# Polysketch attention and a gated FFN on one core: w_out's sums laid over 128 partitions, copies moved behind the sigmoids, and kv joined with neighbouring projections

## The chip, the cores and the metric

The kernel runs on one core of one Trainium2 chip. The metric is the device time of one execution in microseconds (us), as the median of the runs. Engines are named as in the profile: PE is TensorE (PEld its weight loads), ACT is ScalarE, DVE is VectorE, POOL is GpSimd, and SP is the engine that only issues DMAs. A queue letter behind an engine (SPq, ACTq) means its instruction queue. "Lnnn" is a line of the kernel file.

## What is computed

A kernelized attention over 4 batches, 4 heads, 1088 positions and 32 dimensions per head is followed by a feed-forward block with a sigmoid gate. In float32:

```python
def phi(x):                      # 64 features from 32 dimensions, r = 8
    a = np.einsum('rd,bhsd->bhsr', S1, x)
    b = np.einsum('rd,bhsd->bhsr', S2, x)
    return np.einsum('bhsi,bhsj->bhsij', a, b).reshape(*x.shape[:-1], r * r)
q_p, k_p = phi(q), phi(k)
kv = np.einsum('bhsf,bhsd->bhfd', k_p, v)
z = np.sum(k_p, axis=2)
num = np.einsum('bhsf,bhfd->bhsd', q_p, kv)
den = np.einsum('bhsf,bhf->bhs', q_p, z)[..., None] + 1e-06
x = (num / den)                  # reordered to 4352 tokens x 128
gate = 1.0 / (1.0 + np.exp(-(x @ w_gate)))   # 128 x 1536
out = gate * (x @ w_val) @ w_out             # 1536 x 128
```

## The kernel before

**The feed-forward part is the long one.** The 4352 tokens are cut into nine chunks: eight of 512 and a last one of 256. Within a chunk the 1536 hidden columns are cut into twelve blocks of 128. One block of one chunk is a "wave" (`w1`, matmul at L540): the gate and the value projection into one PSUM tile of two banks (pool `psm`, two buffers, tag "wave"), then a sigmoid of the gate half on ACT (L548, into `sg`), then the product of value half and sigmoid on DVE (`glu`, L583; L576 in the last chunk, where one wave holds two blocks). Waves are counted through: chunk 0 has waves 0 to 11, chunk 1 has 12 to 23, and so on; the last chunk has six, from wave 96.

**The second projection.** Chunk 0 multiplies by w_out in the plain way (`w2`, L421), and the last chunk too, with tokens as rows of the result (`w2_end`, L447, `store_end`, L403 and L405). Chunks 1 to 7 are `fast`: a pair of waves and the matching pair of w_out's blocks form a 2 by 2 block product, done with seven half-size products in place of eight (Strassen's scheme in Winograd's form). POOL forms the sums of the activations (`token_sums`, L367, tile `tsum`) and of the weights (`weight_sums`, tile `ws`). `w2_a` issues four products into PSUM bank acc0, `w2_b` three into bank acc1 (L377, both in pool `pso`, one buffer for each bank). They accumulate over the chunk's six pairs. Behind the last pair the banks are summed: ACT copies the upper 64 partitions of a bank to the lower ones (`other`, L473 and L502), DVE adds on 64 partitions (`add`, L479), two transposes (L514) make rows of tokens, and four DMAs (eight where a chunk reaches into the next batch) store them from `o_sb` (L389, on SP). The sum steps are put into the list `moe["late"]`, from which each slot takes one (two in the last chunk).

**The order is written out by hand** for PE, DVE, ACT and POOL (`manual_schedule`, L65): each engine runs what the Python code issues to it, in that order. Only the order of SP's DMAs is chosen by the scheduler. The unit of order is `slot(group, waves)`: it issues an attention step (`group`), then `glu` of the wave before, one entry of `late`, the products that are due (`todo`: `w2_a` three and `w2_b` four waves behind the pair's second wave, each one earlier for the last pair of chunk 7, the flag `early`), and last a new wave with its sigmoid.

**The attention part** of batch 0 runs ahead of the waves. That of batches 1 to 3 is spread over the slots; `plan` gives, for batches 2 and 3, the wave number of each step. `turn_k` and `turn_q` transpose the inputs. `begin` projects keys (`kps`, L673) into the PSUM tile "two" (pool `ps2`, one buffer) and queries (`qcomp`, L819), whose result goes by a DMA on ACT's queue (L837) into a DRAM tile `dq` of one buffer; from there `spread` reads it back with repetition on SP's queue (L844 for the tiles qp and bq, further rows for the tiles a8 and b8). `outer` (L752) makes key features, `sum_z` their sums. `kv_all` is `kv` (L892 and L901, into a PSUM tile "two") and `kvd`, a copy on ACT (L914). `ndt` transposes it on PE (L948, copied at L965), `weights_z` makes the weights of the denominator on DVE (L1001, L1007, L1008), `qmult` (L872) makes query features, and `parts` computes the denominators (`den_j`, L1021) and numerators (L1258), divides, and writes the token columns `xT` that the waves read. `load_kq` and `load_v` fetch the next batch's inputs on SP's queue into the pool `ld`, where one buffer serves kq and bq in turn.

The heart of a slot, as it stands before the change:

```python
            glu()
            for _ in range(2 if moe["ci"] >= len(tok_chk) - 1 else 1):
                if moe["late"]:
                    moe["late"].pop(0)()
            while todo and todo[0][0] <= moe["n"]:
                todo.pop(0)[1]()
            if behind is not None:
                behind()
                behind = None
            if more:
                w1()
```

The end of the program stores the last 256 tokens from two tiles of the ring that `o_sb` uses (pool `sbA`, two buffers):

```python
        o_sb = [sbA.tile([P, P], F32, tag="o_sb", name="o_end") for _ in range(2)]
        for u, copy in enumerate((nc.scalar.copy, nc.vector.tensor_copy)):
            copy(out=o_sb[u], in_=acc[u])
```

Of the kernel before, what the change touches and what calls it, by code (L numbers as in the profile page):

```python
# [16 lines left out]
P = 128  # L17
# [3 lines left out]
def kernel(  # L21
# [24 lines left out]
    NJK = 9  # L46
# [9 lines left out]
    sbN = ctx.enter_context(tc.tile_pool(name="sbN", bufs=1))  # L56
    sbG = ctx.enter_context(tc.tile_pool(name="sbG", bufs=3))

# [288 lines left out]
    moe = {"sum": -1, "ci": 0, "w": 0, "n": 0, "ready": 0, "acc": None, "gate": None, "todo": [], "late": []}  # L347
# [17 lines left out]
    def token_sums(g, t, odd):  # L365
# [48 lines left out]
    def w2(ci, j0, jn, g):  # L414
# [13 lines left out]
        if j0 + jn == NJ:  # L428
            o_sb = sbA.tile([P, 2, TCH // 32, 32], F32, tag="o_sb", name="o_sb")[:, 0]
# [29 lines left out]

    def w2_a(ci, i, g, t):  # L460
# [3 lines left out]
        lo, hi = fst["a"][:64], fst["a"][64:]  # L464
        w, first, last = w_sb[:, 2], i == 0, i == NJ // 2 - 1
        product(lo[:, :HALF], w[:, 2 * i, :64], g[:, 0, :HALF], first, last)
        product(hi[:, :HALF], w[:, 2 * i + 1, :64], g[:, 1, :HALF], first, last)
        product(lo[:, HALF:], ws[:, 3, i], g[:, 1, HALF:], False, last)
        product(hi[:, HALF:], ws[:, 1, i], t[:, 2], False, last)
        if last:  # L470
            e = fst["e"] = raw.tile([P, 2, 2, HALF], F32, tag="w_in", name="other")[:64]
            r = fst["r"] = raw.tile([P, 6, HALF], F32, tag="w_in", name="res")[:64]
            nc.scalar.copy(out=e[:, 0], in_=hi.rearrange("p (u x) -> p u x", u=2))  # L473

            add(ends(r, 1, 3), twice(lo[:, :HALF]), e[:, 0])
            moe["late"] += [lambda: add(r[:, 2], lo[:, HALF:], r[:, 4])]

    def add(out, in0, in1, op=ALU.add):
        nc.vector.tensor_tensor(out=out, in0=in0, in1=in1, op=op)  # L479

    def twice(x):
        return bass.AP(tensor=x.tensor, offset=x.offset, ap=[list(x.ap[0]), [0, 2], [1, HALF]])

    def ends(r, u, step):
        x = r[:, u]
        return bass.AP(
            tensor=x.tensor, offset=x.offset, ap=[list(x.ap[0]), [step * HALF, 2], [1, HALF]]
        )

    def w2_b(ci, i, g, t):  # L490
        if i == 0:
            fst["b"] = pso.tile([P, TCH], F32, tag="acc1", name="prod")
        lo, hi = fst["b"][:64], fst["b"][64:]
        w, first, last = w_sb[:, 2], i == 0, i == NJ // 2 - 1
        p5 = (lo[:, :HALF], ws[:, 0, i], t[:, 0], first, last)
        p4 = (hi[:, :HALF], w[:, 2 * i + 1, 64:], t[:, 3], first, last)
        p7 = ((hi if i % 2 else lo)[:, HALF:], ws[:, 2, i], t[:, 1], False, i >= NJ // 2 - 2)
        for p in (p4, p5, p7) if i % 2 else (p5, p4, p7):
            product(*p)
        if last:  # L500
            e, r = fst["e"], fst["r"]
            nc.scalar.copy(out=e[:, 1], in_=hi.rearrange("p (u x) -> p u x", u=2))  # L502
# [900 lines left out]
```

## Time and profile before

| what | value |
|---|---|
| median of 3 runs | 292.83 us (292.31 to 293.69) |
| the profiled execution's own time | 296.02 us |
| its span in the trace | 294.1 us |
| PE busy | 288.8 us |
| DVE busy | 186.5 us |
| POOL busy | 160.6 us |
| ACT busy | 93.7 us |
| HBM read and written | 20.60 MB and 3.26 MB |
| granted TensorE clock | 0.999 of full |

How to read it: a group line gives the line, engine, operation and tiles, then "busy us, mean ns of one | idle time of that engine just before, and what ended most of it". A timeline line gives start and duration in us, with the engine, the line, the tiles, and in brackets how long the engine had been idle and who released it. Spans of matmuls overlap a little because weight loads and column halves run beside each other. The profiled execution is 1.1% longer than the median; times of single instructions are from it.

### The profile page before, as it was taken

Reading aid. Unit: us, or ns where it says so; the run is one execution under the profiler, and the core shown is the slowest. Engines: PE = TensorE matmul, PEld = TensorE weight load, DVE = VectorE, ACT = ScalarE, POOL = GpSimd, SP = SyncE. Lnnn points to the kernel's source line nnn. Section 1 sums busy time; section 2 is a strip of 40 time slices with the busy share of each in tenths; the row PEclk is TensorE's granted clock in tenths of the full one; section 3 lists DMA queues with packets and bytes.
Section 4 is the critical chain, followed back from the end, with each engine's and each line's share of the span. In section 5 each row is a group of like instructions: output and inputs, shape, how many; then the busy total and the mean of one; then the engine's idle time right before and its main releaser. Section 6 shows DMA issues by size and latency. Waiting matters only on the chain.

```text
span 294.1 us, 5762 instructions
## 1 busy us (share of the span) xinstructions
PE 288.8 (98%) x2264; PEld 156.6 (53%) x2264; DVE 186.5 (63%) x316; ACT 93.7 (32%) x172; POOL 160.6 (55%) x222
## 2 busy tenths in 40 slices
PE   8989999999999999999999999999999999999995
PEld 3543433355455455545555555554555555555895
DVE  5778789885656766677556696667436423552482
ACT  3386542321324222323224222323223223322321
POOL 2266544796535657655456498555456565646300
PEclk9999999999999999999999999999999999999999
DMA  7993613295640168416000474202000200020003
GB/s 219 347 336 68 150 39 125 74 180 137 186 97 0 19 163 159 133 50 177 12 0 2 129 174 106 37 0 38 1 0 2 36 2 0 0 31 7 0 4 54
DMA packets 28890, 24.23 MB, mean 82 GB/s; under 512 B 18560, under 2 KB 24064, under 8 KB 28864
## 3 DMA queue, kind: packets, MB, share of 16 engines
q1 hardware_dynamic: 25808, 21.95, 30.1%
q10 hardware_dynamic: 3056, 1.92, 2.3%
q8 instruction: 18, 0.29, 0.4%
q14 instruction: 8, 0.07, 0.1%
HBM read 20.60 MB, written 3.26 MB: 81 GB/s over the span
## 4 chain that ended last, share of the span: by engine, by line
PE 89%; DMA 7%; SPq 1%; DVE 0%; issue 0%; ACT 0%; DVEq 0%
PE wave L540 55%; PE prod L377 20%; DMA bq<-dq 5%; PE moeout L421 4%; PE moeout L447 2%; PE warm L297 1%; PE kps L673 1%; SPq L844 1%; PE nps L1258 1%; DMA s_in<-in_S_dram 1%; PE kvz L892 1%; PE cqps L819 1%; DMA dq<-cq 1%; DMA b<-dq 1%; PE denj L1021 0%; PE dps L1063 0%
## 5 line engine op out<-in xcount | busy, mean ns | idle before, releaser
L540 PE MATMUL wave<-xT,w_sb 128*64 128x512 f32 (+3 forms) x820 | 210.6, 566 | 0.0
L540 PEld LDWEIGHTS wave<-xT,w_sb 128*64 128x64 f32 (+1 forms) x820 | 85.4, 140 | 63.2 <-issue 51.0
L548 ACT ACTIVATE sg<-wave 128x512 f32<-128x512 f32 x102 | 60.9, 597 | 171.1 <-PE wave L540 163.2
L583 DVE TENSOR_TENSOR g<-wave,sg 128x512 f32<-128x512 f32 x96 | 65.9, 686 | 76.3 <-ACT sg L548 75.0
L367 POOL TENSOR_TENSOR tsum<-g 128x256 f32<-128x256 f32 x84 | 67.9, 810 | 29.7 <-DVE g L583 29.6
L367 POOL TENSOR_TENSOR tsum<-g,tsum 128x256 f32<-128x256 f32 x42 | 34.2, 814 | 57.8 <-DVE g L583 57.6
L377 PE MATMUL prod<-tsum,ws 128*64 128x256 f32 x252 | 62.8, 381 | 0.0
L377 PEld LDWEIGHTS prod<-tsum,ws 128*64 128x64 f32 x252 | 31.2, 137 | 16.0 <-issue 11.8
L377 PE MATMUL prod<-g,w_sb 128*64 128x256 f32 x168 | 34.7, 381 | 0.0
L367 POOL TENSOR_TENSOR tsum<-tsum,g 128x256 f32<-128x256 f32 x42 | 32.7, 779 | 3.3
L377 PE MATMUL prod<-tsum,w_sb 128*64 128x256 f32 x84 | 25.3, 383 | 0.0
L377 PEld LDWEIGHTS prod<-g,w_sb 128*64 128x64 f32 x168 | 16.0, 136 | 17.5 <-issue 14.7
L377 PE MATMUL prod<-g,ws 128*64 128x256 f32 x84 | 25.0, 379 | 0.0
L117 POOL TENSOR_TENSOR head<-head,tail 128x384 int32<-128x384 int32 (+1 forms) x10 | 9.9, 987 | 13.9 <-DVE head L111 12.6
L377 PEld LDWEIGHTS prod<-g,ws 128*64 128x64 f32 x84 | 11.5, 137 | 3.7
L421 PE MATMUL moeout<-g,w_sb 128*128 128x512 f32 (+1 forms) x28 | 12.5, 603 | 0.0
L377 PEld LDWEIGHTS prod<-tsum,w_sb 128*64 128x64 f32 x84 | 10.8, 137 | 3.0 <-issue 2.2
L872 DVE TENSOR_TENSOR qp<-qp,bq 128x1152 f32<-128x1152 f32 (+1 forms) x7 | 9.4, 1344 | 4.6 <-DMA a<-dq 4.6
L752 DVE TENSOR_TENSOR kp<-kab 128x1152 f32<-128x1152 f32 (+2 forms) x10 | 10.9, 1101 | 0.0
L576 DVE TENSOR_TENSOR g<-wave,sg 128x512 f32<-128x512 f32 x6 | 6.7, 1121 | 4.6 <-ACT sg L548 4.6
L479 DVE TENSOR_TENSOR res<-prod,other 64x512 f32<-64x512 f32 (+1 forms) x14 | 7.6, 544 | 3.1 <-DMA a<-dq 1.6
L514 DVE STREAM_TRANSPOSE o_sb<-res 64x512 f32<-64x512 f32 x14 | 9.6, 688 | 0.0
(129 smaller groups left out, 209.6 us busy)
## 6 DMA issues: line engine op xcount, KB each, us to landing
qp<-dq SPq DMA_DIRECT2D x7, 576.0 KB
bq<-dq SPq DMA_DIRECT2D x14, 288.0 KB
kq<-in_k_dram SPq DMA_DIRECT2D x3, 544.0 KB
kq<-in_q_dram SPq DMA_DIRECT2D x3, 544.0 KB
w_in<-in_moe_w_out_dram SPq DMA_DIRECT2D x6, 256.0 KB
w_in<-in_moe_w_gate_dram SPq DMA_DIRECT2D x5, 256.0 KB
w_in<-in_moe_w_val_dram SPq DMA_DIRECT2D x5, 256.0 KB
v<-in_v_dram SPq DMA_DIRECT2D x8, 144.0 KB
```

The source lines that it names most:

```text
L117: nc.gpsimd.tensor_tensor(out=head, in0=head, in1=tail, op=ALU.add)
L367: nc.gpsimd.tensor_tensor(out=t[:, u], in0=in0, in1=in1, op=ALU.subtract)
L377: nc.tensor.matmul(out=out, lhsT=lhsT, rhs=rhs, start=start, stop=stop, skip_group_check=True)
L421: nc.tensor.matmul(out=moe["acc"][d], lhsT=w_sb[:, 2, j, d], rhs=g[:, jj], start=(j == 0), stop=(j == NJ - 1),)
L479: nc.vector.tensor_tensor(out=out, in0=in0, in1=in1, op=op)
L514: nc.vector.transpose(out=o_sb[:64, d].rearrange("p t x -> p (t x)"), in_=r[:, 1 + 2 * d : 3 + 2 * d].rearrange("p u x -> p (u x)"),)
L540: nc.tensor.matmul(out=wv[d, which, jj * tw + o : jj * tw + o + tp], lhsT=w_sb[:, which, j0 + jj, d], rhs=xT[:, t0 + o : t0 + o + tp], sta ...
L548: nc.scalar.activation(out=sg, in_=wv[:, 0], func=ACTF.Sigmoid)
L576: nc.vector.tensor_tensor(out=g.rearrange("p (j u s y) -> p j y u s", j=2, u=2, y=4), in0=wv[:, 1].rearrange("p (j y u s) -> p j y u s", j ...
L583: nc.vector.tensor_tensor(out=g, in0=wv[:, 1], in1=sg, op=MUL)
L752: eng.tensor_tensor(out=KP[b][:, pi, j0:j1].rearrange("p j m (i l) -> p (j m) i l", i=R), in0=bass.AP(tensor=a0.tensor, offset=a0.offset, ...
L872: nc.vector.tensor_tensor(out=q0, in0=q0, in1=half(BQ[b], n), op=MUL)
```

## The change

It has five parts.

1. The seven products go to other halves of the two banks: the sums behind the last pair run on 128 partitions, with the first half of the output columns on the lower 64 and the other half on the upper 64. The copies between partition halves are 64x256 each, made by `cross` on ACT; there are three behind `w2_a`'s last pair, three behind `w2_b`'s, and one of a sum. DVE makes two dependent adds from acc0 (`shared`), two more from acc1 (`first_half`), one for the second half, and one 128x512 transpose. `o_sb` has half its former size. `token_sums` forms t[1] ahead of t[3].
2. The copies are collected in `moe["copies"]` and issued behind the new wave's sigmoid of the slot, in place of ahead of it.
3. The flag `early` goes; a flag `behind` makes the first pair of chunk 1 one wave later.
4. kv of batch 2 is issued into the same PSUM tile as the key projections of batch 3 (`begin(3, 2)`), and kv of batch 3 into the tile of batch 2's last numerators (`parts(2, 3)`). `plan` is replaced by a written-out order, in which batch 3 begins at wave 36 in place of 53 and its parts stand at wave 56 in place of 68; batch 2's begin stands at wave 27 in place of 31.
5. `load_kq(2)` and `load_kq(3)` are issued earlier, into a tile of a new pool that takes the place of `sbN` once that is closed. A warming matmul of 64 columns has 128.

The diff, without blank lines:

```diff
@@
     ld = ctx.enter_context(tc.tile_pool(name="ld", bufs=1))
     sbA = ctx.enter_context(tc.tile_pool(name="sbA", bufs=2))
     raw = ctx.enter_context(tc.tile_pool(name="raw", bufs=NJ // 2))
-    sbN = ctx.enter_context(tc.tile_pool(name="sbN", bufs=1))
     sbG = ctx.enter_context(tc.tile_pool(name="sbG", bufs=3))
+    top = ExitStack()
+    sbN = top.enter_context(tc.tile_pool(name="sbN", bufs=1))
     dram = ctx.enter_context(tc.tile_pool(name="dram", bufs=1, space=bass.MemoryType.DRAM))
@@
     k_t, q_t = {}, {}
+    late_pool = []
     def new_kq(b):
-        t = ld.tile([P, 2 * H * W1], F32, tag="kq", name="kq")
+        pool, tag, w = (ld, "kq", 2 * H * W1) if b < 2 else (late_pool[0], "kq2", 2 * T * D)
+        t = pool.tile([P, w], F32, tag=tag, name="kq")
         kq = t[:, : 2 * T * D].rearrange("p (a t d) -> p a t d", a=2, t=T)
         k_t[b], q_t[b] = kq[:, 0], kq[:, 1]
@@
     xT = const.tile([P, NTOK], F32, tag="xT")
-    moe = {"sum": -1, "ci": 0, "w": 0, "n": 0, "ready": 0, "acc": None, "gate": None, "todo": [], "late": []}
+    moe = {"sum": -1, "ci": 0, "w": 0, "n": 0, "ready": 0, "acc": None, "gate": None, "todo": [], "late": [], "copies": []}
     def fast(ci):
         return 0 < ci < len(tok_chk) - 1 and tok_chk[ci][1] == TCH
@@
             sub(0, g[:, 0, HALF:], g[:, 0, :HALF])
             return
         sub(2, g[:, 1, HALF:], t[:, 0])
-        sub(3, t[:, 2], g[:, 1, :HALF])
         sub(1, g[:, 1, HALF:], g[:, 0, HALF:])
+        sub(3, g[:, 1, :HALF], t[:, 2])
     def product(out, lhsT, rhs, start, stop):
         nc.tensor.matmul(
...
@@
     fst = {}
     def w2_a(ci, i, g, t):
         if i == 0:
             moe["sum"] = ci
             fst["a"] = pso.tile([P, TCH], F32, tag="acc0", name="prod")
-        lo, hi = fst["a"][:64], fst["a"][64:]
+        ps = fst["a"]
+        lo, hi = ps[:64], ps[64:]
         w, first, last = w_sb[:, 2], i == 0, i == NJ // 2 - 1
         product(lo[:, :HALF], w[:, 2 * i, :64], g[:, 0, :HALF], first, last)
-        product(hi[:, :HALF], w[:, 2 * i + 1, :64], g[:, 1, :HALF], first, last)
+        product(hi[:, :HALF], ws[:, 1, i], t[:, 2], first, last)
         product(lo[:, HALF:], ws[:, 3, i], g[:, 1, HALF:], False, last)
-        product(hi[:, HALF:], ws[:, 1, i], t[:, 2], False, last)
+        product(hi[:, HALF:], ws[:, 2, i], t[:, 1], False, last)
         if last:
-            e = fst["e"] = raw.tile([P, 2, 2, HALF], F32, tag="w_in", name="other")[:64]
-            r = fst["r"] = raw.tile([P, 6, HALF], F32, tag="w_in", name="res")[:64]
-            nc.scalar.copy(out=e[:, 0], in_=hi.rearrange("p (u x) -> p u x", u=2))
-            add(ends(r, 1, 3), twice(lo[:, :HALF]), e[:, 0])
-            moe["late"] += [lambda: add(r[:, 2], lo[:, HALF:], r[:, 4])]
-    def add(out, in0, in1, op=ALU.add):
-        nc.vector.tensor_tensor(out=out, in0=in0, in1=in1, op=op)
-    def twice(x):
-        return bass.AP(tensor=x.tensor, offset=x.offset, ap=[list(x.ap[0]), [0, 2], [1, HALF]])
-    def ends(r, u, step):
-        x = r[:, u]
-        return bass.AP(
-            tensor=x.tensor, offset=x.offset, ap=[list(x.ap[0]), [step * HALF, 2], [1, HALF]]
-        )
+            e = fst["e"] = raw.tile([P, 4, HALF], F32, tag="w_in", name="other")
+            r = fst["r"] = raw.tile([P, 3, HALF], F32, tag="w_in", name="res")
+            cross(e[:64, 0], hi[:, :HALF])
+            cross(e[64:, 0], lo[:, :HALF])
+            cross(e[:64, 1], lo[:, :HALF])
+            def shared():
+                add(r[:, 0], ps[:, :HALF], e[:, 0])
+                add(r[:, 0], ps[:, HALF:], r[:, 0])
+                cross(e[64:, 1], r[64:, 0])
+            moe["late"] += [shared]
+    def cross(out, in_):
+        moe["copies"].append(lambda: nc.scalar.copy(out=out, in_=in_))
+    def add(out, in0, in1):
+        nc.vector.tensor_tensor(out=out, in0=in0, in1=in1, op=ALU.add)
     def w2_b(ci, i, g, t):
         if i == 0:
             fst["b"] = pso.tile([P, TCH], F32, tag="acc1", name="prod")
-        lo, hi = fst["b"][:64], fst["b"][64:]
+        ps = fst["b"]
+        lo, hi = ps[:64], ps[64:]
         w, first, last = w_sb[:, 2], i == 0, i == NJ // 2 - 1
-        p5 = (lo[:, :HALF], ws[:, 0, i], t[:, 0], first, last)
+        p5 = (lo[:, HALF:], ws[:, 0, i], t[:, 0], False, last)
         p4 = (hi[:, :HALF], w[:, 2 * i + 1, 64:], t[:, 3], first, last)
-        p7 = ((hi if i % 2 else lo)[:, HALF:], ws[:, 2, i], t[:, 1], False, i >= NJ // 2 - 2)
-        for p in (p4, p5, p7) if i % 2 else (p5, p4, p7):
+        out2 = hi[:, HALF:] if i % 2 else lo[:, :HALF]
+        p2 = (out2, w[:, 2 * i + 1, :64], g[:, 1, :HALF], first, i >= NJ // 2 - 2)
+        for p in (p4, p5, p2) if i % 2 else (p2, p4, p5):
             product(*p)
         if last:
             e, r = fst["e"], fst["r"]
-            nc.scalar.copy(out=e[:, 1], in_=hi.rearrange("p (u x) -> p u x", u=2))
-            o_sb = sbA.tile([P, 2, TCH // 32, 32], F32, tag="o_sb", name="o_sb")
-            def fifth_seventh():
-                add(ends(r, 2, 3), twice(lo[:, :HALF]), ends(r, 2, 2))
-                add(r[:, 0], lo[:, HALF:], e[:, 1, 1])
-            def last_sums():
-                add(r[:, 3], r[:, 4], e[:, 1, 0], op=ALU.subtract)
-                add(r[:, 3:5], ends(r, 3, 2), twice(r[:, 0]))
-            def turned(d):
+            cross(e[:64, 2], lo[:, HALF:])
+            cross(e[64:, 2], lo[:, HALF:])
+            cross(e[:64, 3], hi[:, HALF:])
+            o_sb = sbA.tile([P, TCH // 32, 32], F32, tag="o_sb", name="o_sb")
+            def first_half():
+                add(r[:, 1], ps[:, :HALF], e[:, 1])
+                add(r[:64, 1], r[:64, 1], e[:64, 3])
+            def turn_store():
                 nc.vector.transpose(
-                    out=o_sb[:64, d].rearrange("p t x -> p (t x)"),
-                    in_=r[:, 1 + 2 * d : 3 + 2 * d].rearrange("p u x -> p (u x)"),
-                )
-            def turn_store():
-                turned(1)
-                store(ci, lambda g4: o_sb[32 * (g4 % 2) : 32 * (g4 % 2) + 32, g4 // 2])
-            moe["late"] += [fifth_seventh, last_sums, lambda: turned(0), turn_store]
+                    out=o_sb.rearrange("p t x -> p (t x)"),
+                    in_=r[:, 1:3].rearrange("p u x -> p (u x)"),
+                )
+                store(ci, lambda g4: o_sb[32 * g4 : 32 * g4 + 32])
+            moe["late"] += [first_half, lambda: add(r[:, 2], r[:, 0], e[:, 2]), turn_store]
     def w1():
@@
             token_sums(pair, moe["t"], odd)
             if odd:
                 part = (ci, j0 // 2, pair, moe["t"])
-                early = ci == len(tok_chk) - 2 and j0 == NJ - 1
-                todo.append((n + 3 - early, lambda: w2_a(*part)))
-                todo.append((n + 4 - early, lambda: w2_b(*part)))
+                behind = ci == 1 and j0 == 1
+                todo.append((n + 3 + behind, lambda: w2_a(*part)))
+                todo.append((n + 4 + behind, lambda: w2_b(*part)))
         moe["gate"] = glu
         moe["w"] += 1
@@
                 behind = None
             if more:
                 w1()
-            elif not todo:
+            for copy in moe["copies"]:
+                copy()
+            moe["copies"] = []
+            if more:
+                continue
+            if not todo:
                 break
             else:
                 todo.pop(0)[1]()
@@
     WD = 160
     mask = {}
-    def kps(b):
+    def kps(b, also=None):
         t = ps2.tile([P, 2, 512], F32, tag="two", name="kps")
+        if also is not None:
+            kv(also, ZS[also], t[:, 0, NJK * 32 : NJK * 32 + 2 * F])
         ts = [t[:, 0], t[:, 1]]
         turns = [(g, pi) for g in range(4) for pi in range(2)]
...
@@
                     skip_group_check=True,
                 )
-    def kv(b, zsum):
-        kvz = KVZ[b] = ps2.tile([P, 2, 512], F32, tag="two", name="kvz")[:, 0]
+    def kv(b, zsum, kvz=None):
+        if kvz is None:
+            kvz = ps2.tile([P, 2, 512], F32, tag="two", name="kvz")[:, 0]
+        KVZ[b] = kvz
         for j in [1, 2, 3, 4, 5, 6, 7, 8, 0]:
             for h in range(H):
                 nc.tensor.matmul(
@@
         start=True,
         stop=True,
     )
-    warm(64)
+    warm(128)
     st_ = st_[:, : 2 * R].rearrange("p (n r) -> p n r", n=2)
     sk = const.tile([P, 2, 2, R], F32, tag="sk")
     nc.vector.tensor_tensor(
@@
     slot(None, 1)
     cq = {}
-    def begin(b):
+    def begin(b, also=None):
         glu()
-        kps(b)
+        kps(b, also)
+        if also is not None:
+            moe["copies"].append(lambda: kvd(also))
         cq[b] = qcomp(b, (0, 1), (psm, "wave"))
         spread(b, (0, 1), cq[b], nc.scalar, nc.sync)
@@
                     stop=True,
                 )
-    def parts(b):
+    def parts(b, also=None):
         den_j(b)
         glu()
         t = psm.tile([P, 2, 512], F32, tag="wave", name="nps")
         numerators(b, t, False)
         num = sbA.tile([P, 2, NJK, 2, F], F32, tag="kp", name="num", bufs=1)
         num = num.rearrange("p c j m f -> p (c j m f)")[:, :1024].rearrange("p (c w) -> p c w", c=2)
-        nc.scalar.copy(out=num, in_=t)
+        first = t
         t = ps2.tile([P, 2, 512], F32, tag="two", name="nps2")
         numerators(b, t[:, :, WD : WD + 32], True)
+        if also is not None:
+            kv(also, ZS[also], t[:, 1, 4 * F : 6 * F])
+        nc.scalar.copy(out=num, in_=first)
         turn_den(b, den_i(b, t[:, 0, :WD]))
+        if also is not None:
+            moe["copies"].append(lambda: kvd(also))
         for n in range(2):
             rb = sbA.tile([P, 9, 2, 32], F32, tag="rb", name="rb")
             t0, tn = q_chk[n]
@@
     load_kq(1)
     slot(None, 1)
     slot(lambda: part01(lambda: narrow_w(NJ - 1, 3)), 1)
+    top.close()
+    late_pool.append(ctx.enter_context(tc.tile_pool(name="late", bufs=1)))
     slot(last01, 1)
     load_v(1)
+    load_kq(2)
     turn_k(1)
     slot(None, 1)
     turn_q(1, 0)
@@
     slot(lambda: ndt(1), 1)
     slot(None, 1)
     qmult(1, 1)
-    load_kq(2)
     slot(None, 1)
     slot(lambda: parts(1), 1)
     moe["store"]()
@@
     def until(n):
         slot(None, n - moe["n"])
-    plan = {2: (27, 29, 30, 31, 32, 34, 36, 37, 38, 39, 42, 44)}
-    plan[3] = (48, 49, 51, 53, 56, 57, 58, 59, 60, 61, 63, 68)
-    for b in range(2, B):
-        at = iter(plan[b])
-        until(next(at))
-        turn_k(b)
-        for n in range(2):
-            until(next(at))
-            turn_q(b, n)
-        until(next(at))
-        slot(lambda: begin(b), 1)
...
-        until(next(at))
-        slot(lambda: kv_all(b), 1)
-        if b + 1 < B:
-            load_v(b + 1)
-        until(next(at))
-        qmult(b, 0)
-        slot(lambda: ndt(b), 1)
-        weights_z(b)
-        until(next(at))
-        qmult(b, 1)
-        load_kq(b + 1)
-        until(next(at))
-        slot(lambda: parts(b), 1)
+    def features(b, *at):
+        steps = [(outer, 0), (outer, 1), (sum_z, 0), (sum_z, 1)]
+        for n, (step, i) in zip(at, steps):
+            until(n)
+            step(b, i)
+    until(24)
+    turn_k(2)
+    until(25)
+    turn_q(2, 0)
+    until(26)
+    turn_q(2, 1)
+    load_kq(3)
+    until(27)
+    slot(lambda: begin(2), 1)
+    features(2, 28, 29, 31, 32)
+    until(34)
+    turn_k(3)
+    until(35)
+    turn_q(3, 0)
+    turn_q(3, 1)
+    until(36)
+    slot(lambda: begin(3, 2), 1)
+    load_v(3)
+    until(37)
+    weights_z(2)
+    outer(3, 0)
+    until(38)
+    slot(lambda: ndt(2), 1)
+    outer(3, 1)
+    until(40)
+    qmult(2, 0)
+    until(41)
+    sum_z(3, 0)
+    until(42)
+    sum_z(3, 1)
+    until(44)
+    qmult(2, 1)
+    until(45)
+    slot(lambda: parts(2, 3), 1)
+    until(48)
+    weights_z(3)
+    slot(lambda: ndt(3), 1)
+    until(50)
+    qmult(3, 0)
+    until(52)
+    qmult(3, 1)
+    until(56)
+    slot(lambda: parts(3), 1)
     slot(None, 10**3)
```

More of the change, by code (lines that the diff above doesn't have):

```diff
@@ L428, in w2 @@
         if j0 + jn == NJ:
-            o_sb = sbA.tile([P, 2, TCH // 32, 32], F32, tag="o_sb", name="o_sb")[:, 0]
+            o_sb = sbA.tile([P, TCH // 32, 32], F32, tag="o_sb", name="o_sb")
             nc.vector.transpose(out=o_sb.rearrange("p t d -> p (t d)"), in_=moe["acc"])
@@ L501, in w2_b @@
             e, r = fst["e"], fst["r"]
-            nc.scalar.copy(out=e[:, 1], in_=hi.rearrange("p (u x) -> p u x", u=2))
-            o_sb = sbA.tile([P, 2, TCH // 32, 32], F32, tag="o_sb", name="o_sb")
-            def fifth_seventh():
-                add(ends(r, 2, 3), twice(lo[:, :HALF]), ends(r, 2, 2))
-                add(r[:, 0], lo[:, HALF:], e[:, 1, 1])
-            def last_sums():
-                add(r[:, 3], r[:, 4], e[:, 1, 0], op=ALU.subtract)
-                add(r[:, 3:5], ends(r, 3, 2), twice(r[:, 0]))
-            def turned(d):
+            cross(e[:64, 2], lo[:, HALF:])
+            cross(e[64:, 2], lo[:, HALF:])
+            cross(e[:64, 3], hi[:, HALF:])
+            o_sb = sbA.tile([P, TCH // 32, 32], F32, tag="o_sb", name="o_sb")
+            def first_half():
+                add(r[:, 1], ps[:, :HALF], e[:, 1])
+                add(r[:64, 1], r[:64, 1], e[:64, 3])
+            def turn_store():
                 nc.vector.transpose(
-                    out=o_sb[:64, d].rearrange("p t x -> p (t x)"),
-                    in_=r[:, 1 + 2 * d : 3 + 2 * d].rearrange("p u x -> p (u x)"),
-                )
-            def turn_store():
-                turned(1)
-                store(ci, lambda g4: o_sb[32 * (g4 % 2) : 32 * (g4 % 2) + 32, g4 // 2])
-            moe["late"] += [fifth_seventh, last_sums, lambda: turned(0), turn_store]
+                    out=o_sb.rearrange("p t x -> p (t x)"),
+                    in_=r[:, 1:3].rearrange("p u x -> p (u x)"),
+                )
+                store(ci, lambda g4: o_sb[32 * g4 : 32 * g4 + 32])
+            moe["late"] += [first_half, lambda: add(r[:, 2], r[:, 0], e[:, 2]), turn_store]
     def w1():
@@ L852, in spread @@
         put = get
-        B8[b] = sbA.tile([P, W1], F32, tag="b8", name="b8", bufs=1)
-        A8[b] = sbA.tile([P, 2, WD], F32, tag="a8", name="a8", bufs=1)
+        pool = late_pool[0] if b == B - 1 else sbA
+        B8[b] = pool.tile([P, W1], F32, tag="b8", name="b8", bufs=1)
+        A8[b] = pool.tile([P, 2, WD], F32, tag="a8", name="a8", bufs=1)
         for x in range(2):
@@ L1340, in until @@
         slot(None, n - moe["n"])
-    plan = {2: (27, 29, 30, 31, 32, 34, 36, 37, 38, 39, 42, 44)}
-    plan[3] = (48, 49, 51, 53, 56, 57, 58, 59, 60, 61, 63, 68)
-    for b in range(2, B):
-        at = iter(plan[b])
-        until(next(at))
-        turn_k(b)
-        for n in range(2):
-            until(next(at))
-            turn_q(b, n)
-        until(next(at))
-        slot(lambda: begin(b), 1)
-        for pi in range(2):
-            until(next(at))
-            outer(b, pi)
-        for step in range(2):
-            until(next(at))
-            sum_z(b, step)
-        until(next(at))
-        slot(lambda: kv_all(b), 1)
-        if b + 1 < B:
-            load_v(b + 1)
-        until(next(at))
-        qmult(b, 0)
-        slot(lambda: ndt(b), 1)
-        weights_z(b)
-        until(next(at))
-        qmult(b, 1)
-        load_kq(b + 1)
-        until(next(at))
-        slot(lambda: parts(b), 1)
+    def features(b, *at):
[46 more added lines that the diff above has]
+    slot(lambda: parts(3), 1)
     slot(None, 10**3)
```

## Prediction

> **What bounds the kernel now.** I read the page's busy table and chain first, then its costliest groups, then what TensorE (PE) waits for, then the timeline of the three engines around one boundary between token chunks, and last the tail.
>
> ```profile
> PE 288.8 (98%) x2264; PEld 156.6 (53%) x2264; DVE 186.5 (63%) x316; ACT 93.7 (32%) x172; POOL 160.6 (55%) x222
> ...
> PE 89%; DMA 7%; SPq 1%; DVE 0%; issue 0%; ACT 0%; DVEq 0%
> ...
> L548 ACT ACTIVATE sg<-wave 128x512 f32<-128x512 f32 x102 | 60.9, 597 | 171.1 <-PE wave L540 163.2
> L583 DVE TENSOR_TENSOR g<-wave,sg 128x512 f32<-128x512 f32 x96 | 65.9, 686 | 76.3 <-ACT sg L548 75.0
> ```
>
> PE is busy 98% of 294.1 us and carries 89% of the chain; the sigmoid waits for the wave, the GLU multiply (glu) for the sigmoid. What PE itself waited for:
>
> ```profile
> PE warm L297 <- PEq L1387: 0.8, 1, 0.8
> PE denj L1021 <- DMA b<-dq: 0.4, 1, 0.4
> PE ndps L948 <- ACT kvd L914: 0.4, 1, 0.4
> PE nps L1082 <- ACT nd L965: 0.4, 1, 0.4
> ```
>
> These are 2.0 us in all, once each. So less work on DVE or ACT is worth nothing by itself: a change pays only if it takes work or a mode change off PE, and costs wherever it makes PE wait. The boundary of chunk 5 to 6, on PE, ACT and DVE in turn (start, duration):
>
> ```profile
> 222.44 0.65 PE L377 MATMUL prod<-g,w_sb 128*64 128x256 f32 x4
> ...
> 223.31 1.94 PE L540 MATMUL wave<-xT,w_sb 128*64 128x512 f32 x8
> 225.09 0.40 PE L377 MATMUL prod<-tsum,ws 128*64 128x256 f32 x1
> ```
>
> ```profile
> 220.51 0.60 ACT L548 ACTIVATE sg<-wave 128x512 f32<-128x512 f32 x1 [1.11 <-PE wave L540]
> 221.13 0.58 ACT L502 COPY other<-prod 64x512 f32<-64x512 f32 x1
> ```
>
> ```profile
> 221.21 0.69 DVE L583 TENSOR_TENSOR g<-wave,sg 128x512 f32<-128x512 f32 x1 [1.09 <-ACT sg L548]
> 221.82 0.41 DVE L479 TENSOR_TENSOR res<-prod,res 64x256 f32<-64x256 f32 x1
> ...
> 224.53 0.41 DVE L479 TENSOR_TENSOR res<-prod,other 64x256 f32<-64x256 f32 x1
> ```
>
> The first product of the new chunk (222.44) overwrites acc0. It starts 1.93 us after the sigmoid at 220.51, and the last reader of acc0 (the add at 221.82) ended at 222.23: cover of 0.2 us, no wait. acc1 is freed by the add that ends at 224.94, its product starts at 225.09: a hand-over from DVE to PE takes 0.15. The wave ahead, 1.71 from 223.31, ended at 225.02, so PE lost 0.07. The tail:
>
> ```profile
> 290.94 0.29 DVE L403 COPY o_end<-moeout 128x128 f32<-128x128 f32 x1 [1.71 <-PE moeout L447]
> ```
>
> ```profile
> 290.50 0.27 ACT L403 COPY o_end<-moeout 128x128 f32<-128x128 f32 x1 [2.44 <-PE moeout L447]
> 290.80 0.63 ACTq L405 DMA_DIRECT2D out_dram<-o_end  x1
> ```
>
> ```profile
> 291.26 0.64 SPq L405 DMA_DIRECT2D out_dram<-o_end  x1
> ```
>
> Two end tiles leave side by side on two queues, 2.84 us from the last issue to the end of the span.
>
> **What the Trainium skill says.** "PSUM — Partial Sum Buffer", Engine vs sequencer instructions: the queues of ScalarE and VectorE are strict FIFO and matmuls start in program order. The trace agrees (glu stands behind whatever was issued ahead of it), and this is what decides below. "VectorE: DVE Perf Modes", The DRAIN you can't avoid: the next op waits for the pipe to empty. For a dependent add the trace agrees (a second one starts 0.44 us after the first, of 0.41); for independent ones the pitch is less (glu at 221.21, next at 221.82). "TensorEngine Tiling (Array Packing)", Key Properties: a change of tiling mode drains the array. The trace agrees in direction: the inserted steps of one batch cost 0.3 to 0.4 us above their streaming time (kv 1.41 against 1.07).
>
> **1. Sums over 128 partitions: PE.** Seven products of the same size stay, in the same pairs of column halves: 0. DVE's sums per chunk fall from about 5.1 us (0.68+0.41+0.67+3x0.41+1.0 of adds, rounded, and two transposes of 0.69) to 2.7 (five adds near 0.41, one 128x512 transpose 0.69); DVE is idle 37%, so 0.
>
> **2. acc0 at a chunk boundary.** ACT now makes three 64x256 copies behind the sigmoid, and the last reader of acc0 is the second of two dependent adds, which needs the third copy. No such copy is in the trace: nearest are kvd (128x256, 0.37) and nd (128x128, 0.26), so 0.26 to 0.37; I take 0.37 with a pitch of 0.28 (back-to-back ACT ops start some 0.09 before the last one's end). Counted from the sigmoid's start (next ACT op 0.50 later, as sg 124.02 to nd 124.52): the third copy ends at 0.50+2x0.28+0.37 = 1.43. First add 1.48 to 1.89, second 1.92 to 2.33, hand-over 0.15: acc0 is free at 2.48. PE is there at 1.93: **wait 0.55**. Bounds 0.2 (short copies) to 0.8 (hand-overs of 0.15 between ACT and DVE too). Where the column halves of PE run skewed part of it is taken up, about 0.33; I take 0.45 on average. There are six boundaries to a fast chunk; at the one where begin(2) now stands (chunk 1 to 2), its matmuls of about 1.3 us in the same slot hide it. 5 x 0.45 = **+2.25** (1.0 to 4.0).
>
> **3. Last chunk.** The early issue of the last pair's products goes; w2_end's first product needs acc0 behind a glu of 1.12 (L576) in place of 0.69: free at 0.63+1.04 for glu, then the adds to 2.55, hand-over 0.15, so 2.7 against 1.93: **+0.75** (0.3 to 1.0).
>
> **4. acc1.** Its last reader is now the first of the sums' second half, issued one slot earlier than its need: the stall of 0.07 goes at six or seven boundaries: **-0.5**.
>
> **5. kv joined.** kv(2) goes ahead of kps(3) into one PSUM tile, kv(3) into parts(2): two insertions less, 0.3 each (0 to 0.5): **-0.6**. What their other orders cost: kvd's copy comes behind sigmoid 36, and weights_z(2) with outer(3,0) are now queued on DVE *ahead of* glu(36). From that sigmoid's start: kvd ends 0.87, three small ops of weights_z take 1.14 (125.66 to 126.80), outer 1.25, glu 0.69: it ends near 4.0, with hand-over 4.15. Wave 38 waits for glu(36), which reads its PSUM buffer; PE is there after 1.93 + ndt 0.3 + products 0.86 = 3.1. Queued behind it: everything on PE. **+0.95** (0.6 to 1.3). Elsewhere in waves 39 to 45 I count a margin of 0.3 to 0.5, so 0.
>
> **6. The tail.** o_sb's tiles are halved, and in the changed program the pool gives both end tiles the same address: the DVE copy waits for ACT's copy and for the landing of ACT's DMA. Issue 290.80 plus about 2.1 (the put of dq, issued 54.60, released its first reader at 56.71) = 292.9; copy 0.06+0.29, SP's issue 0.03 later at 293.3 in place of 291.26: **+2.0** (1.5 to 2.7). Nothing covers the tail.
>
> **7. DMAs.** load_kq(2) and (3) are issued earlier, on SP's queue, into a pool of their own. load_kq(2), 1.1 MB at some 46.6, lands in about 4 us (load_kq(1) took that), ahead of the put of 54.6, in a stretch where the DMA queues are empty: 0. The a/b rows for denj of batch 1 keep their 0.4 wait. SP passes chunk 1's stores behind the b rows of spread(2): nobody waits for stores until o_sb comes round. spread(3)'s put on ACT must wait until spread(2) has read dq (one buffer): nine slots, about 24.7 us, against 20 to 22 for the earlier spreads: margin near 3, less load_kq(3)'s 4 us of sharing. Taken at 0; up to +4 if late, as ACT's sigmoids stand behind the put. warm(64) becomes warm(128): +0.05.
>
> **Sum.** +2.25+0.75-0.5-0.6+0.95+2.0+0.05 = +4.9 us. The profiled execution, 296.02 (span 294.1), would become 300.9 (span 299.0); it stands 1.1% above the median 292.83, which is what I forecast from: 292.83+4.9 = **297.7**.
>
> **The rivals.**
> - *The copies hide and the joins win (other side).* If the third copy ends by 0.9 after the sigmoid (copies of about 0.15 at their pitch), acc0 is free at 1.93 and step 2 and 3 fall to 0. For it: ACT is idle 68%; against: no ACT copy of this trace is under 0.26. Even so the tail's 2.0 stays unless ACT's DMA is seen landed by 291; both needed: -0.5-0.6+0 = 291.7. Decided by those two.
> - *Only one half comes true*: the tail alone (2.0-1.1+0.95 = 294.7), or the stalls with a tail of nothing (295.7).
> - *dq's single buffer holds ACT at put(3)*: for it, load_kq(3) shares the queues just as spread(2) begins; against, about 3 us of margin. +2 to +4: 300 to 301.5.
> - *Nothing measurable*: stalls absorbed by skew down to 1.0+0.3, wave 38 at 0, tail 1.5, joins -1.1: +1.7, 294.5, just outside; within needs one thing more.
>
> **How the numbers follow.** 0.5% (1.46 us) is about what a measurement of this kernel can tell from no change. Forecast and its bounds 0.65, one half only 0.12, dq 0.1, nothing measurable 0.09, other side 0.04. So faster 0.04, same 0.1 (with the edge of "one half"), slower 0.86. Low end 294.0: the low bounds of all steps (294.5) and the half cases; high end 301.0: stalls near their upper bounds (about +7.5) or dq late.
>
> **What would show it.** In the changed profile: PE's list of waits has lines "prod <- DVE" near 0.3 to 0.6 each, five or six times, and one "wave <- DVE" near 0.9 at wave 38; the DVE end copy starts about 2 us after PE's end; SP's last issue lies 2 us behind ACT's; no wait of ACT at a dq put. Wrong if PE shows no such waits, if the end copies stand side by side, or if the insertions of kv cost what they did.

## The result, and the profile after

The changed kernel takes 301.09 us (300.06 to 301.21), the kernel before 292.83: 2.8% slower, ratio 1.0276 with a 95% interval of 1.0254 to 1.0299. The loss is 8.3 us; 4.9 were forecast, and the median lies just beyond the upper end of the range, 301.0. The profiled execution took 300.06 us, its span is 298.3. A few executions of several kernels below had a granted TensorE clock of about 0.988 and took some 3 us more (in e1 three at 0.989 took 301.8 to 303.4 us, three at 0.999 to 1.0 took 298.8 to 299.3); why the clock was lower is not shown.

The page of the changed kernel, its busy times and the chain that ended last:

```profile
PE 286.7 (96%) x2264; PEld 155.8 (52%) x2264; DVE 173.6 (58%) x302; ACT 103.7 (35%) x207; POOL 158.6 (53%) x222
...
PE 93%; ACT 3%; DVE 2%; DMA 1%; issue 0%; POOL 0%; DVEq 0%
```

DVE has 12.9 us less to do and ACT 10.0 more, PE as many instructions as before, and PE now idles 4% of its span where it idled 2%. The chain carries ACT (3%) and DVE (2%), which it did not before. What PE waited for (total, times, longest):

```profile
PE prod L381 <- ACT sg L554: 2.6, 4, 0.7
PE warm L301 <- PEq L1431: 0.8, 1, 0.8
PE moeout L451 <- ACT sg L554: 0.6, 1, 0.6
PE prod L381 <- DVE res L497: 0.5, 2, 0.3
...
PE wave L546 <- DVE g L589: 0.2, 1, 0.2
```

Six waits of products and one of `moeout` are new. The releaser "ACT sg" is a wrong name: the timeline shows it. The boundary of chunk 5 to 6 again, on PE, ACT and DVE:

```profile
222.70 0.40 PE L381 MATMUL prod<-g,w_sb 128*64 128x256 f32 x1 [0.65 <-ACT sg L554]
```

```profile
219.89 0.60 ACT L554 ACTIVATE sg<-wave 128x512 f32<-128x512 f32 x1 [2.00 <-PE prod L381]
220.52 1.12 ACT L494 COPY other<-prod 64x256 f32<-64x256 f32 x3
```

```profile
221.67 0.42 DVE L497 TENSOR_TENSOR res<-prod,other 128x256 f32<-128x256 f32 x1 [0.39 <-ACT other L494]
222.13 0.42 DVE L497 TENSOR_TENSOR res<-prod,res 128x256 f32<-128x256 f32 x1
```

Read it from the sigmoid at 219.89. The three copies run from 220.52 to 221.64, the first add waits for the third, the second add ends at 222.55, and PE's first product into acc0 starts 0.15 later, at 222.70, after 0.65 us of nothing. That is 2.81 us behind the sigmoid, where it was 1.93. The tail, on DVE, ACT and SP:

```profile
295.06 0.29 DVE L407 COPY o_end<-moeout 128x128 f32<-128x128 f32 x1 [3.94 <-DMA out_dram<-o_end]
```

```profile
292.36 0.27 ACT L407 COPY o_end<-moeout 128x128 f32<-128x128 f32 x1 [2.38 <-PE moeout L451]
292.66 0.63 ACTq L409 DMA_DIRECT2D out_dram<-o_end  x1
```

```profile
295.38 0.64 SPq L409 DMA_DIRECT2D out_dram<-o_end  x1
```

DVE's end copy waits for the landing of ACT's DMA, which reads the same buffer; SP's issue is 2.7 us behind ACT's, where it was 0.46.

**Where the time went.** The start of every sigmoid marks a wave, so the ACT timelines give the length of each stretch (us). "Before, again" is the kernel before with another tail (experiment e6), "mended" is e7:

| stretch | before | before, again | changed | sums alone (e4) | mended (e7) |
|---|---|---|---|---|---|
| start to wave 0 | 19.40 | 16.71 | 16.72 | 17.18 | 16.54 |
| waves 0 to 12 | 32.49 | 32.50 | 32.49 | 32.49 | 32.49 |
| waves 12 to 24 | 34.54 | 33.56 | 34.11 | 33.94 | 33.95 |
| waves 24 to 72 | 128.98 | 128.97 | 131.47 | 131.54 | 129.16 |
| waves 72 to 96 | 59.51 | 59.52 | 61.13 | 61.13 | 59.34 |
| waves 96 to 101 | 12.54 | 12.54 | 13.46 | 13.46 | 12.54 |
| wave 101 to the end | 6.69 | 8.65 | 8.89 | 8.89 | 6.68 |

The trace of before, on which the forecast rests, began 2.7 us late and lost 1.0 us more at wave 22, where denj waits for a DMA; neither is seen in its second trace. That is why the two profiled executions differ by only 4.0 us. From wave 0 on, with the second value for waves 12 to 24, the kernel before takes 273.8 us and the changed one 281.6: 7.8 us, and all stretches but the first two hold a share of it.

### The profile page after: what moved, and what is told of

Same layout as the page of the kernel before. It is cut to its first block, busy times and chain, and to the rows that moved or that the text cites. A ratio compares the mean times of both kernels' runs of the same rounds, so it can differ in the third digit from the quotient of the medians.

```text
span 298.3 us, 5776 instructions
## 1 busy us (share of the span) xinstructions
PE 286.7 (96%) x2264; PEld 155.8 (52%) x2264; DVE 173.6 (58%) x302; ACT 103.7 (35%) x207; POOL 158.6 (53%) x222
## 4 chain that ended last, share of the span: by engine, by line
PE 93%; ACT 3%; DVE 2%; DMA 1%; issue 0%; POOL 0%; DVEq 0%
PE wave L546 58%; PE prod L381 21%; PE moeout L425 4%; PE warm L301 2%; PE moeout L451 2%; ACT sg L554 1%; PE nps L1276 1%; PE kps L686 1%; ACT other L494 1%; PE cqps L832 1%; DMA out_dram<-o_end 1%; DVE kp L765 1%; PE denj L1037 1%; PE nps L1098 0%; DVE res L497 0%
## 5 line engine op out<-in xcount | busy, mean ns | idle before, releaser
L371 POOL TENSOR_TENSOR tsum<-g,tsum 128x256 f32<-128x256 f32 x84 | 67.8, 807 | 60.8 <-DVE g L589 60.5
L371 POOL TENSOR_TENSOR tsum<-g 128x256 f32<-128x256 f32 x84 | 66.6, 793 | 36.0 <-DVE g L589 35.8
L381 PE MATMUL prod<-tsum,ws 128*64 128x256 f32 x252 | 68.2, 382 | 0.0
L381 PE MATMUL prod<-g,w_sb 128*64 128x256 f32 x168 | 50.2, 380 | 3.1 <-ACT sg L554 2.6
L381 PEld LDWEIGHTS prod<-g,w_sb 128*64 128x64 f32 x168 | 22.2, 137 | 31.6 <-issue 24.2
L381 PEld LDWEIGHTS prod<-tsum,ws 128*64 128x64 f32 x252 | 32.0, 136 | 8.9 <-issue 6.2
L494 ACT COPY other<-prod 64x256 f32<-64x256 f32 x42 | 15.4, 366 | 0.6
L497 DVE TENSOR_TENSOR res<-prod,other 128x256 f32<-128x256 f32 x14 | 5.9, 420 | 6.2 <-ACT other L494 6.2
L301 PE MATMUL warm<-const-float32-1.0 128*128 128x512 f32 (+2 forms) x12 | 6.9, 704 | 0.8 <-PEq L1431 0.8
```

Of the source, the lines that this page charges most:

```text
L301: nc.tensor.matmul(out=t[:, 0, :n], lhsT=x, rhs=r, start=True, stop=True)
L371: nc.gpsimd.tensor_tensor(out=t[:, u], in0=in0, in1=in1, op=ALU.subtract)
L381: nc.tensor.matmul(out=out, lhsT=lhsT, rhs=rhs, start=start, stop=stop, skip_group_check=True)
L494: moe["copies"].append(lambda: nc.scalar.copy(out=out, in_=in_))
```

## The experiments

Times are medians; the kernel before, run on the same chip beside each group, took 292.5 to 292.9.

**e1: a buffer for each end tile.**

```diff
-        o_sb = [sbA.tile([P, P], F32, tag="o_sb", name="o_end") for _ in range(2)]
+        o_sb = [sbA.tile([P, P], F32, tag=f"o_end{u}", name="o_end", bufs=1) for u in range(2)]
```

> The changed kernel, but its two end tiles have a buffer each. Theory (the shared address of the end tiles costs the tail 2.3 us in the trace): 2.3 us less than the changed kernel, about 298.8, with DVE's end copy back right behind PE. Rival (another transfer, the stores of the chunk before, ends last anyway): less than 0.5 us gained.

Measured: 300.53 us, but from 298.81 to 303.37, three runs below 299.3 and three above 301.8, so the median decides nothing. The three below, at the full granted clock, are what was expected. The trace agrees: the last stretch fell from 8.89 to 6.63 us, and DVE's end copy stands right behind PE again, as before:

```profile
293.99 0.29 DVE L407 COPY o_end<-moeout 128x128 f32<-128x128 f32 x1 [1.67 <-PE moeout L451]
```

The shared buffer costs 2.3 us. This trace also has a pause of PE in the middle of wave 45 (PE's timeline) that the trace of the changed kernel lacks:

```profile
142.50 1.02 PE L546 MATMUL wave<-xT,w_sb 128*64 128x512 f32 x4
144.29 0.65 PE L546 MATMUL wave<-xT,w_sb 128*64 128x512 f32 x2 [0.76 <-issue]
```

"issue" says that PE waited for nothing that the profile shows. The step from wave 44 to 45 took 6.66 us here, 6.69 in e2, 6.55 in e3, and 5.80 in the profiled execution of the changed kernel, the fastest of its five runs.

**e6: the same from the other side.** The kernel before, with one buffer for both end tiles (tag "o_end", bufs=1).

> The kernel before, but its two end tiles share one buffer, as they do in the changed kernel. Theory: 2.3 us slower than the kernel before, 295.2, with DVE's end copy about 4 us behind PE's last matmul. Rival (something else in the changed kernel delays the end): less than 0.5 us slower. The rest of its trace is that of the kernel before once more, and shows what of that trace was chance.

Measured: 294.74 us, ratio 1.0086 (1.0055 to 1.0118): +1.9. In its trace the last stretch grew from 6.69 to 8.65, and all other stretches equal those of before but for the two pieces of chance named above.

```profile
289.25 0.29 DVE L403 COPY o_end<-moeout 128x128 f32<-128x128 f32 x1 [3.71 <-DMA out_dram<-o_end]
```

So the tail is settled in both directions: 2.0 to 2.3 us in the traces.

**e2: the copies out of acc0 ahead of the sigmoid.** In `w2_a`:

```diff
-            cross(e[:64, 0], hi[:, :HALF])
-            cross(e[64:, 0], lo[:, :HALF])
-            cross(e[:64, 1], lo[:, :HALF])
+            nc.scalar.copy(out=e[:64, 0], in_=hi[:, :HALF])
+            nc.scalar.copy(out=e[64:, 0], in_=lo[:, :HALF])
+            nc.scalar.copy(out=e[:64, 1], in_=lo[:, :HALF])
```

> The changed kernel, but the three copies out of acc0 are issued at once, ahead of the slot's sigmoid; the adds stay in the next slot. Theory (the third copy behind the sigmoid holds acc0): the adds then follow glu directly, acc0 is free about 0.54 us earlier at five chunk boundaries, nearly nothing at the last chunk, where glu takes 1.12: about 298.4. Rival (the two dependent adds behind glu are the whole cost): no change, 301. Rival (the copies now delay the sigmoid): slower than 301.

Measured: 299.04 us (298.78 to 299.07). The steps at waves 52, 64, 76 and 88 fell by 0.46 to 0.48 us each, the one at wave 100 by 0.13; the step at wave 45 rose by 0.89 with PE's pause. At the boundary (DVE, then PE):

```profile
221.19 0.41 DVE L497 TENSOR_TENSOR res<-prod,other 128x256 f32<-128x256 f32 x1
221.64 0.42 DVE L497 TENSOR_TENSOR res<-prod,res 128x256 f32<-128x256 f32 x1
```

```profile
222.21 0.40 PE L381 MATMUL prod<-g,w_sb 128*64 128x256 f32 x1 [0.17 <-DVE res L497]
```

The adds now follow glu directly, and half of the wait is gone. The other half is the adds' place behind glu.

**e3: the adds ahead of glu too.**

```diff
-            moe["late"] += [shared]
+            shared()
```

> As the kernel with the copies out of acc0 ahead of the sigmoid, and the two adds that read acc0 are issued to DVE at once too, ahead of that slot's glu. The sums run on 128 partitions as in the change. Theory (only the place of these instructions costs, not the sums over 128 partitions): PE's wait at all boundaries and before the last chunk's first product goes, 4.0 + 0.9 us: about 296.1. Rival (the sums as such cost PE time): no less than 299.

Measured: 295.61 us (294.86 to 296.53), ratio 1.0085 to the kernel before (1.0054 to 1.0115). All waits at the boundaries are gone (ACT, DVE, then PE, at the same boundary; this run is some 2 us ahead):

```profile
216.84 0.37 ACT L484 COPY other<-prod 64x256 f32<-64x256 f32 x1
217.77 0.60 ACT L554 ACTIVATE sg<-wave 128x512 f32<-128x512 f32 x1 [0.57 <-PE prod L381]
```

```profile
217.70 0.42 DVE L497 TENSOR_TENSOR res<-prod,res 128x256 f32<-128x256 f32 x1
```

```profile
219.70 0.38 PE L381 MATMUL prod<-g,w_sb 128*64 128x256 f32 x1
```

The last reader of acc0 ends at 218.12, 1.6 us before PE writes it. Each undisturbed chunk takes 29.67 us per 12 waves: 0.09 less than before, where the changed kernel took 30.56. The sums over 128 partitions cost nothing; the place of five instructions did.

**e4: the sums alone** (the kernel before with parts 1 to 3 of the change and the longer warming matmul).

> The kernel before with the new sums alone: products, copies behind sigmoids, adds, the two flags and the halved o_sb; plan, kv and loads as before. Theory (the sums with their tail are the whole loss, the joins come out near nothing): 4.0 + 0.9 + 2.3 us above the kernel before, 300.0. Rival (the joined kv and the new order cost several us of the 8.3): 297 or less.

Measured: 300.60 us (300.22 to 301.57), ratio 1.0256. Nearly the whole loss is there without one joined kv. The 0.5 us to the changed kernel's median is not clear of noise: its interval is 1.0254 to 1.0299, that of e4 1.0212 to 1.0299.

**e5: the joins alone** (the kernel before with parts 4 and 5 but for the warming matmul). Part 5 has one step more than the diff ahead of the forecast prints: the tiles a8 and b8 of batch 3 lie in the new pool too.

> The kernel before with parts 4 and 5 of the change alone: kv joined, the new order, the earlier loads. Theory (the joins save little and give it back in PE pauses): 0.2 to 1.0 us above the kernel before, 293.1 to 293.9. Rival (the joins pay as forecast, -0.6, with the wait at wave 38 small): 292.3. Rival (they are the rest of the loss): 295 or more.

Measured: 294.36 us (294.10 to 294.76), ratio 1.0056 (1.0038 to 1.0074): +1.5, more than the theory said and less than the last rival. Its trace names two places: denj's DMA wait at wave 22 (0.7, which the kernel before also has in one of its two traces), and a new one at wave 43 (DVE, then PE):

```profile
129.52 1.10 DVE L483 TENSOR_TENSOR res<-res 64x512 f32<-64x512 f32 x1
...
132.66 0.83 DVE L940 TENSOR_TENSOR zs<-zs,kp 64x256 f32<-64x256 f32 x1
133.41 0.67 DVE L587 TENSOR_TENSOR g<-wave,sg 128x512 f32<-128x512 f32 x1
```

```profile
134.14 1.94 PE L544 MATMUL wave<-xT,w_sb 128*64 128x512 f32 x8 [0.74 <-DVE g L587]
```

The old sums (1.10 us on 64 partitions) and the sum of batch 3's features meet in DVE's queue ahead of glu. With the lighter new sums the step at wave 43 takes 2.22 us (e7) in place of 3.16. The two halves of the change are not independent: the denser order needs the lighter sums.

**e7: both mends in the changed kernel** (edits of e1, e2 and e3).

> The changed kernel with both mends: copies and adds out of acc0 ahead of the sigmoid and glu, and a buffer for each end tile. Theory (the two losses add): 295.6 - 2.3 = 293.3, that is 0.4 above the kernel before. Rival (a third cause of over 1 us is left): above 294.5.

Measured: 293.24 us (292.33 to 293.77), ratio 1.0011 (0.9999 to 1.0024). The two losses add, 7.9 us in all, and no third cause of over 1 us is left.

**e8: the mended sums with the old plan** (e4 with the same edits).

> The kernel before with the new sums on 128 partitions, but copies and adds out of acc0 ahead of the sigmoid and glu and a buffer for each end tile; plan and kv as before. Theory (the sums themselves are free and worth nothing): 300.6 - 2.3 - 5.7 = 292.6, no change against the kernel before. Rival (less DVE work pays by itself): 291.5 or less.

Measured: 292.66 us, ratio 1.0000 (0.9985 to 1.0015). Freed of its two faults, the new way to sum is worth nothing that can be measured, though DVE is busy 175.3 us in place of 186.5. In the traces this nothing is a sum of two: waves 24 to 96 gain 0.35 us, and waves 12 to 24 lose 0.38 to the later first pair of chunk 1 (33.94 against 33.56).

**e9, e10, e11: kv apart again, in the mended kernel.** kv of batch 3 at wave 44 (e9), kv of batch 2 at wave 35 (e10), both (e11):

```diff
     qmult(2, 1)
+    slot(lambda: kv_all(3), 1)
     until(45)
-    slot(lambda: parts(2, 3), 1)
+    slot(lambda: parts(2), 1)
```

```diff
+    slot(lambda: kv_all(2), 1)
     until(36)
-    slot(lambda: begin(3, 2), 1)
+    slot(lambda: begin(3), 1)
```

> The mended kernel, but kv of batch 3 has its own tile and its own place, wave 44, just ahead of parts of batch 2. Theory (PE pauses inside wave 45 because of the long run of matmuls ahead of it, and the join saves less than that): the pause of 0.5 to 0.9 at wave 45 goes, an insertion of about 0.3 comes: 292.8 to 293.2. Rival (the join saves 0.3 as forecast and the pause comes from something else): 293.6. Rival (the pause comes from the transfers of the spread of batch 3, which go on): it is seen at wave 44 or 45 again.

> The mended kernel, but kv of batch 2 has its own tile and its own place, wave 35, ahead of begin of batch 3. Theory of the forecast (a join saves a mode change's 0.3): 293.5. Rival (it saves nothing, since the steps at waves 36 to 39 together took no less than apart): 293.2 or less.

> The mended kernel with both kv apart, in the new order of the batches. If the joins save 0.3 each: 293.8. If they save nothing and parts with kv costs a pause: 292.5 to 293.0. Either way it tells the order of the batches apart from the joins.

Measured: e9 292.48 us (292.29 to 292.86), ratio 0.9988 (0.9974 to 1.0002); e10 293.69 (293.10 to 296.23), ratio 1.0040 (1.0023 to 1.0057); e11 292.82 (292.58 to 296.89), ratio 1.0013 (0.9985 to 1.0042). In the traces, kv(2) apart lengthens waves 35 to 43 by 0.29 us (e10 against e7) and 0.28 (e11 against e9): that join saves what was forecast. kv(3) apart adds 1.40 at wave 44 and takes 1.89 from wave 45: that join costs 0.5. Joined parts and kv without the pause (5.80 less a plain step of 2.56) take 3.24 us, those apart (1.40 + 4.36 - 2.56) 3.20. So it saves nothing by itself, and a pause of up to 0.9 comes with it.

**e12: without the flag `behind`** (e9, with the first pair of chunk 1 at its usual waves).

> The mended kernel with kv of batch 3 apart, and without the flag that makes the first pair of chunk 1 one wave later. In the traces waves 12 to 24 took 33.95 us with that flag and 33.56 in a kernel without it: if the flag costs this, 0.4 less than the kernel with kv of batch 3 apart, about 292.1, just below the kernel before. Rival (the flag only shifts work; the difference comes from POOL's weight sums, which the first pair then waits for): 292.5 or more.

Measured: 293.23 us (292.97 to 293.77), ratio 1.0016 (1.0006 to 1.0027): slower than with the flag. The theory fell. PE and POOL in its trace:

```profile
58.53 0.43 PE L381 MATMUL prod<-tsum,ws 128*64 128x256 f32 x1 [1.07 <-POOL tsum L371]
```

```profile
56.71 1.77 POOL L371 TENSOR_TENSOR tsum<-g 128x256 f32<-128x256 f32 x1
```

`w2_a` now needs two of POOL's token sums, and not POOL's weight sums, as the rival had it, but the second token sum comes late. It ran beside DVE's sum_z (1.21 us from 56.69) and took 1.77 us; where no DVE instruction ran beside it, the same operation took 0.72 in this trace. The Trainium skill, "SBUF — State Buffer", section SBUF: two separate sides, gives a reason: a DVE op with two SBUF inputs and a GpSimd op that reads SBUF share a port pair, which the one that starts first holds for its whole length. The trace fits: sum_z started 0.02 ahead of POOL, and 1.77 is near the 1.19 that were left of it plus 0.72. With the flag the token sum is just as slow (1.77 in e9), but PE asks for it a wave later. Waves 12 to 24 take 33.95 us with the flag (e9) and 34.86 without (e12), against 33.56 in the kernel before: the flag saves 0.9 in the new kernel, and 0.4 is left.

## Why the prediction was right or wrong

It was right in its direction and in the three places that it named, and too low by 3.4 us. By its steps, with measured values from the table of stretches:

| step | forecast | measured | how |
|---|---|---|---|
| 1 sums as such | 0 | 0 | e8, ratio 1.0000, the last row's 0.4 in it |
| 2 and 4, acc0 and acc1 at boundaries | +1.75 | +4.2 | sums alone less before: waves 24 to 72, 2.57; 72 to 96, 1.61 |
| 3 last chunk | +0.75 | +0.9 | 13.46 - 12.54 |
| 5 joins and their waits | +0.35 | -0.1 to +0.8 | changed less sums alone, waves 24 to 72: -0.07; with the pause of 0.87 seen in e1: +0.8 |
| 6 tail | +2.0 | +2.0 to +2.3 | e6, e1; 2.2 in the changed kernel's trace |
| 7 loads, warming | +0.05 | not told apart | |
| first pair of chunk 1 later (flag `behind`) | not costed | +0.4 | waves 12 to 24, 33.94 - 33.56 |

**The step that failed is step 2, a term mis-sized.** "The third copy ends at 0.50+2x0.28+0.37 = 1.43", "acc0 is free at 2.48". The copies took the 0.37 that was chosen, but the first began 0.63 after the sigmoid's start and they followed each other every 0.37 (1.12 for three), so the third ended at 1.75 and PE started at 2.81. The lines that the forecast shows had this start: the copy at 221.13 stands 0.62 behind the sigmoid at 220.51. I took the start and the pitch from another pair, sg and nd. Then the wait was multiplied down: "where the column halves of PE run skewed part of it is taken up, about 0.33; I take 0.45 on average". Nothing was taken up. The idle time is 0.65, and the first product also loses the 0.23 by which it used to start ahead of the wave's end: the step lengthened by 0.93, and two later steps gave back 0.06 each. 0.81 per chunk, as the stretch of waves 72 to 84 has it (30.56 - 29.75), is 0.8 where 0.45 less 0.08 stood.

That at begin(2) "its matmuls of about 1.3 us in the same slot hide it" was half wrong too: in the sums alone, with the old plan, the step at wave 28 is 0.61 longer than before, and in the changed kernel the one at wave 29, behind begin(2), has 0.56 that e3 does not have.

**Step 4 was right in kind**: the mended chunks are 0.09 us shorter than before.

**Step 5 came near by luck: two of its errors have opposite signs, and the pause was not in it.** The wait at wave 38 was to be 0.95 (its own terms give 1.0) and is 0.2. On DVE in the changed kernel:

```profile
118.21 0.22 DVE L1017 TENSOR_TENSOR zz<-kvd,unit 128x64 f32<-128x64 f32 x1 [3.21 <-ACT kvd L930]
...
118.86 1.35 DVE L765 TENSOR_TENSOR kp<-kab 128x1152 f32<-128x1152 f32 x1
```

weights_z takes 0.65 from 118.21 to 118.86, not 1.14: the zz of 0.63 that I priced it with (125.66 in the trace of before) is 0.22 here. The saving of 0.3 holds for kv(2) (0.28 and 0.29) and not for kv(3) (0). One more sum is off without effect: the terms of DVE's old sums in step 1 add up to 5.4, not 5.1.

**Step 6 was right**, in mechanism and size: from ACT's issue to DVE's copy, which waits for the landing, it is 2.4 us (292.66 to 295.06) and 2.1 in e6 (287.13 to 289.25), against the 2.1 read off the put of dq.

**The rivals.** That the copies hide is refuted, as is a hold at the put of dq: in the trace of the changed kernel that put is issued at 115.31, right behind its copy (114.64 to 115.28). The pause of PE at wave 45 was in no rival. It goes with kv joined into parts, though not in every execution: it is in e1, e2, e3, e7 and e10, not in the changed kernel's own trace nor in e5. Without that join (e4 with the old plan, e9 and e11 with the new one) it is not seen, though in e9 and e11 the spread of batch 3 runs on just the same. So those transfers alone do not make it.

The traces hold a lead to what PE waits for. The page of e1 lists a DMA queue named "instruction" with 18 packets of 16 KB in the whole execution. Two of them fall between 139 and 146 us (the DMA view of that window):

```profile
q8 instruction: 2, 0.03, 2.2%
```

Count the matmuls and weight loads that PE has started when a packet starts, and number the packets from 0. In all 14 traces packet n starts at 256n plus 153 to 332, with one exception; so the queue seems to fetch PE's program, 256 of these instructions to a packet. The exception is the packet near wave 45 in the kernels with kv(3) joined. In the five traces with the pause it starts at 256n plus 427 to 435, and PE goes on 2.3 to 2.6 us after its start. In the two without the pause it starts a little sooner, at 336 (the changed kernel) and 367 (e5), and PE reaches the same matmul 2.8 and 2.6 us later and does not stop. With kv(3) apart it starts at 274 to 286. So PE most likely stood without instructions: the long run of small matmuls outran the fetch of the program. No run moved the fetch alone, and why it starts late is open.

**The difference of the medians**, 8.3 us, is then 4.2 + 0.9 + 2.2 + 0.4, which is 7.7, and the rest, about 0.5, probably joins with their pause (301.09 against 300.60 for the sums alone, a difference within the noise of the two). The best kernel of the study, e9, has 292.48 us against 292.53 before: no difference that can be told.

## What to carry to other kernels

On an engine that is busy 98%, an instruction on an idle engine is free only until it is the last reader of a buffer that the busy engine writes next: ask of every moved copy which buffer it holds, and count from the event it now waits behind to the write. An edit that shrinks a tile can change the addresses of its ring: look at who shares one at the very end, where nothing covers a wait. Take the distance between two instructions from the same pair in the trace, not from a pair that looks like it, and do not discount a wait by a cover that no row shows.

## What the runs showed of the hardware

- ACT's copies on 64 partitions, two of which change partition half while the third stays in the lower one, did not overlap. Three 64x256 copies from PSUM took 1.12 us, 0.37 each and one every 0.38, and the first began 0.63 after the start of a sigmoid of 0.60; a 128-partition copy (nd) began 0.50 after one. The Trainium skill, "ScalarE: Activation LUTs", section What ACT_TABLE_LOAD costs, says that back-to-back ACTIVATEs overlap by about 93 ns; the trace agrees for sg and nd (0.10) and not for these copies. Whether the change of partition half is the reason was not tried.
- DVE's adds on 128 partitions took as long as those on 64 (0.42 against 0.41 for 256 columns), while 512 columns on 64 partitions took 0.67 (an input from PSUM) to 1.10 (both from SBUF).
- PE can pause inside a wave for up to 0.76 us with no wait that the profile shows, in five of seven traces with kv(3) joined into parts and in none of the others. The five are those in which the 16 KB packet that seems to hold PE's program starts latest (at 256n plus 427 to 435 matmuls and weight loads, elsewhere at most 367).
